# Banks from the waves' tiles, whole copies of the weights across halves, batch 3's turnings two waves later, and sums over x in two groups, in a polysketch-attention and GLU kernel

## Chip, cores and metric

The kernel runs on one core of a Trainium2 chip. The metric is the device time of one execution in microseconds (us). The median of three runs of the kernel before is 292.66 us (291.77 to 294.08).

## The reference

Four batches of four heads, 1088 positions, head width 32, fp32. Attention without a softmax over sketched features, and then a gated feed-forward block on the result:

```
def phi(x):
    a = np.einsum('rd,bhsd->bhsr', S1, x)
    b = np.einsum('rd,bhsd->bhsr', S2, x)
    return np.einsum('bhsi,bhsj->bhsij', a, b).reshape(*x.shape[:-1], r * r)
q_p, k_p = (phi(q), phi(k))
kv = np.einsum('bhsf,bhsd->bhfd', k_p, v)
z = np.sum(k_p, axis=2)
num = np.einsum('bhsf,bhfd->bhsd', q_p, kv)
den = np.einsum('bhsf,bhf->bhs', q_p, z)[..., None] + 1e-06
...
gate = 1.0 / (1.0 + np.exp(-(x @ w_gate)))
val = x @ w_val
return (gate * val @ w_out).astype(np.float32)
```

x is the attention's output `num / den`, 4352 tokens of 128 features; `w_gate` and `w_val` are 128 x 1536, `w_out` is 1536 x 128.

## The kernel before

**Tokens and waves.** x lies transposed in on-chip memory as `xT` (128 features x 4352 tokens), cut into eight chunks of 512 tokens and one of 256. Chunks 0 to 4 are done in 60 *waves*, twelve a chunk, numbered 0 to 59. A wave (`w1`, L615) multiplies one chunk by 128 columns of the gate weights and 128 of the value weights: eight TensorE records (L630) into one accumulation tile `wave` of 128 x 2 x 512 (two banks: bank 0 holds the gate, bank 1 the value). ScalarE takes the sigmoid of bank 0 (`sg`, L638) and VectorE multiplies it with bank 1 (`g`, L665). The product with `w_out` is done for chunks 1 to 4 in seven products instead of eight (Strassen's way), two waves later and more: `w2_a` and `w2_b` (their matmuls have line L478, as all that go through `product`), which need sums over tokens that GpSimd makes (`token_sums`, L468). There are two `wave` tiles, so the wave after next waits until this one's `g` is done.

**Attention beside the waves.** The attention of batches 1 to 3 is laid between the waves by hand. `slot()` issues one wave, `until(n)` issues waves until number n, and `plan[b]` (L1416) holds for batch b the wave numbers at which its twelve steps are issued: the turnings of k and q (`turn_k`, L725, and two of `turn_q`), the sketches (`begin`, whose first matmuls are `kps`, L756), the outer products, sums for z, `kv_all`, the denominators and `parts`, which writes x of that batch (`xT`, L1367). `begin` also spreads the features over partitions by a long ladder of transfers on SyncE's queue (`a<-dq`, `b<-dq`, L948), each of which is issued when the transfer eight before it has landed. Other small work hangs on `moe["prep"]`, a list of (wave, function) popped in order after each wave.

**Weights across.** `cross_weights` (L414) makes the weight combinations for the seven-product form of the first products. It copies pieces of the gate and value weights from one half of the partitions to the other, in seven transfers of 192 KB on ScalarE's queue (`fw<-w_sb`, L446, at `LOAD_AT`), and then adds and subtracts on VectorE (L441, at `SUM_AT`). It is called after wave 22, when the counter stands at 23, so that every entry up to 23 is popped at one time, after wave 23.

**The section.** Chunks 5, 6 and 7 are the *section* (`section()`, L1468): also the gate and value products are done in seven products there. Before it, x is loaded into `yt` with both halves on both halves of the partitions (`load_y`, four transfers of 128 KB on SyncE's queue, L1456) and four differences over x are made on GpSimd (`x_sum`, L1466); for chunk 5 that is at waves 54 and 56 to 59. `section` closes the pools of the wave tiles (four banks) and of a tile `two` (two banks) and opens a pool `pg` with six tiles of one bank, b0 to b5. Six gated pairs a chunk, 18 in all (w = 0 to 17), even and odd ones in their own banks: GA = b0 and b4, GC = b1 and b5, V = b2 and b3. The work is written out by hand as a string `ORDER` of 698 items, issued from left to right:

- `P1:w` to `P7:w`, and with an apostrophe for the second 128 columns: the seven products of pair w. P1 and P2 add into GA, P5 and P3 into GC, P6, P7 and P4 into V. Each uses half of TensorE's rows.
- `Aa`, `Ac` (ScalarE, L1555 and L1557) copy GA into V and GC into `s5`; `Sa`, `Sc` (ScalarE, L1559, L1561) are the sigmoids of GA and GC; `D1` adds V and `s5` into GC, `D2` adds V and `s5` into `c2` (VectorE, L570); `M1`, `M2` multiply V and `c2` with the sigmoids (VectorE, L1567, L1569). In pair w: P1 (both) before Aa; P5 (both) before Ac; Aa before P6; P6 before D1; P2 before Sa; P7 before D2; P3 and D1 before Sc; P4 before M1.
- `Q`: GpSimd's sums of g over tokens (L1582). `T`: differences over x for the next chunk. `WLA`, `WUA`, `WLB`, `WUB`: products with `w_out` on the lower or upper half of the rows; `WF` on all of them.
- `EA`, `EB` (L1584): ScalarE copies a finished accumulation bank (L1593), and five transfers on SyncE's queue (L1595 to L1600) move quarters of it. `F0` to `F5` add them up, `F6` turns and stores (L490).
- `C`, `Y`, `Z`, `O`: the last chunk of 256 tokens: C the products (Y reads GA, Z reads GC), Y the sigmoid (L1632), Z the multiplication (L1634), O the product with `w_out`.

The program is run in the order in which it is written; each engine takes its own instructions in that order, and what an instruction waits for on other engines is worked out by the compiler from the tiles that it reads and writes.

Of the kernel before, what the change touches and what calls it, by code (L numbers as in the profile page):

```python
# [16 lines left out]
P = 128  # L17

ORDER = """
P1:1 P1:0 T2:1 P1':0 WUB:-2.0 P5:1 WLA:-2.1 P5:0 P1':1 Aa:0 P5':0 P5':1 Aa:1 P2':0 P6':0 P2:0 P6:0  # L20
Ac:0 P6':1 P2:1 Ac:1 D1:0 P2':1 P6:1 Sa:1 D1:1 P3:0 P7:0 P3':0 P7':0 Sa:0 P7':1 P3':1 D2:0 T0:1 P7:1
P3:1 P1:2 P4':0 Sc:1 D2:1 P1':2 P4:0 Sc:0 P4:1 P1:3 M1:0 P1':3 P4':1 P5':3 P5':2 Aa:2 M1:1 P5:3
WLA:-1.1 P6:2 P5:2 M2:0 Aa:3 P6':2 P2:2 Ac:2 P2:3 P6':3 Q0:0 P6:3 WUB:-1.1 Ac:3 D1:2 WLA:-1.0
WUB:-1.0 Q1:0 D1:3 P2':3 WLA:-2.0 P2':2 P7':2 Sa:3 M2:1 P3:2 P7:2 Sa:2 P3':3 P3':2 D2:2 Q0:1 P3:3
P7':3 Sc:2 P1:5 P7:3 Q1:1 Sc:3 P4:2 P1':4 D2:3 P1:4 P4':2 Q2:0 P5:4 P1':5 M1:2 P4':3 WUA:-1.0 Q2:1
WUA:-2.1 P4:3 M2:3 Aa:4 P5':5 P5':4 WLB:-1.1 P6:4 M1:3 Q0:3 Ac:4 P2':4 P6':4 Aa:5 WUA:-1.1 WLB:-2.0
Q3:1 D1:4 P2:4 WUA:-2.0 P5:5 P6:5 M2:2 T1:1 EA:-1 P6':5 P7:4 Sa:4 P7':4 P3:4 Q0:2 P2':5 P3':4 Ac:5
D2:4 P2:5 P1:6 Q3:0 Sc:4 WLB:-1.0 WUA:1.1 D1:5 P4':4 P1':6 Sa:5 Q1:2 M2:4 P4:4 P5:6 EB:-1 P7:5
WUA:0.0 Q1:3 M1:4 P7':5 WUA:1.0 P5':6 P3':5 Q2:3 D2:5 Aa:6 P3:5 WLB:1.0 WLB:0.0 WUA:0.1 Ac:6 T3:1
F0:-1 P6:6 P4:5 Sc:5 Q3:3 WLB:1.1 P6':6 P4':5 P1':7 D1:6 Q0:4 P2':6 P5':7 P2:6 P1:7 M1:5 Q2:2 P7:6  # L30
P3:6 M2:5 Aa:7 WLA:0.1 P7':6 Q3:2 P3':6 P5:7 Sa:6 F1:-1 P2:7 P6':7 Ac:7 D2:6 WUB:1.1 P6:7 T0:2 P1':8
P2':7 Sc:6 D1:7 P1:8 WUB:3.0 T2:2 Sa:7 WLA:1.0 P4:6 M2:6 P3':7 P7:7 T1:2 P7':7 P3:7 P4':6 WLA:3.1
Q1:4 Sc:7 D2:7 P1':9 WLA:0.0 WUB:0.0 P5':8 M1:6 P4:7 P1:9 Q0:6 M2:7 Aa:8 P4':7 P5:9 P5:8 WUB:1.0
Q0:5 M1:7 WLA:3.0 P5':9 Ac:8 WLA:1.1 P6:8 F2:-1 Q1:5 Aa:9 P6':8 WLA:2.0 WUB:3.1 WLA:2.1 Ac:9 D1:8
Q2:5 P6:9 P2':9 WUB:2.0 P6':9 Q2:4 P3:8 P7':8 D1:9 P7:8 P3':8 T3:2 P2':8 P2:9 Sc:8 D2:8 P7':9 P3':9
Q3:4 Sa:9 P3:9 P2:8 M2:8 P4':8 P7:9 Q0:7 Sa:8 WLB:3.1 P4:8 D2:9 Sc:9 WUA:2.0 WLB:2.0 Q3:5 P1:10
WUA:2.1 M1:8 Q1:7 P4:9 P5:11 M2:9 P4':9 P5':11 P1:11 P1':10 M1:9 WLB:5.0 WUA:3.1 Aa:10 WLB:4.0
WUA:3.0 F3:-1 Ac:11 P5':10 P1':11 F4:-1 P5:10 P6:10 Aa:11 WUA:5.1 WLB:3.0 Ac:10 P6':10 WLB:5.1 Q0:9
P6':11 WUA:4.1 D1:10 WUA:4.0 P2:10 Q2:7 P2':10 WUA:5.0 F5:-1 P6:11 P7':10 Q1:6 Sa:10 P3:10 P7:10
D1:11 P2':11 P3':10 Q3:7 P1:12 WUB:5.1 D2:10 Sc:10 WUB:4.0 P7:11 Q1:9 P2:11 P7':11 M2:10 Q2:6 P4':10  # L40
WLA:5.0 Sa:11 P4:10 WLA:4.0 D2:11 WUB:5.0 WLA:5.1 Q3:6 M1:10 P1:13 WLA:4.1 EB:0 P3:11 P4':11 Q0:10
EA:0 P3':11 P4:11 WUB:7.1 P1':12 Sc:11 M1:11 Q1:10 WUB:6.0 P5':12 Aa:12 P1':13 P5:12 M2:11 Q2:9
P5:13 WLA:6.0 Aa:13 P6:12 WLA:7.1 F6:-1 Q3:9 Ac:12 WLA:7.0 P6':12 P5':13 WLA:6.1 Q0:8 D1:12 P6:13
P2':13 Ac:13 WUB:7.0 P6':13 F0:0 Q0:11 P3':12 P7':12 D1:13 P3:12 P7:12 Q2:10 P2:12 P2:13 Sc:12 D2:12
P3:13 P2':12 Q3:10 Sa:13 P3':13 P7':13 M2:12 P7:13 P4:12 Q1:11 Sa:12 WLB:6.0 P4':12 D2:13 Sc:13
WUA:6.0 WLB:7.1 Q1:8 WUA:6.1 P1:14 M1:12 WUA:7.1 P4':13 Q2:8 M2:13 P4:13 P5':15 P1':14 P1:15 Q2:11
M1:13 P1':15 P5':14 Aa:14 WUA:9.0 WLB:7.0 Q3:11 F1:0 Aa:15 P5:14 WUA:10.0 WLB:10.0 P6:14 Q3:8 Ac:14
P2:14 P6':14 P5:15 P6:15 D1:14 P6':15 WUA:9.1 Ac:15 WUA:7.0 P2':14 F2:0 P3:14 P7:14 D1:15 Sa:14
Q0:13 P7':14 P3':14 WUA:8.0 WLB:11.1 Q0:12 Sc:14 D2:14 WLB:9.1 WUA:8.1 WUA:11.1 WLB:11.0 Q1:13 M2:14
WLB:9.0 P4:14 WLB:8.0 P4':14 Q2:13 WUA:10.1 P7':15 M1:14 P3':15 P7:15 Q1:12 WUA:11.0 P1':16 D2:15  # L50
P5:16 P3:15 Q2:12 P2':15 P1:16 F3:0 Sc:15 P2:15 P4':15 F4:0 Q3:12 WUB:8.0 P4:15 F5:0 Sa:15 P5':17
WLA:8.0 Q3:13 Aa:16 WUB:9.1 WLA:8.1 WLA:9.0 P5:17 M1:15 P6:16 P5':16 Ac:17 WLA:10.0 P6':16 M2:15
Ac:16 WLA:11.1 P1:17 P1':17 WLA:9.1 D1:16 WUB:9.0 WLA:11.0 Aa:17 WUB:11.0 WLA:10.1 Q0:15 P3':16
P7':16 EA:1 P6:17 P7:16 Q1:15 P2:17 P6':17 D2:16 P3:16 WUB:10.0 Q0:14 P2':16 P2':17 D1:17 Sc:16
P2:16 P4:16 Q2:15 P4':16 WLA:12.0 M2:16 Sa:16 P7:17 WUB:11.1 Q1:14 Sa:17 P3':17 WLA:13.0 M1:16 P3:17
P7':17 Q0:16 C1:0 Sc:17 D2:17 Q2:14 C0:0 C3:0 M2:17 Y:0 Q1:16 C2:0 EB:1 C1:1 Z:0 Q0:17 P4:17
WUA:13.0 WLB:12.0 WUA:13.1 Q2:16 F6:0 WUA:12.0 WLB:13.1 WUA:12.1 WLB:13.0 Q3:14 F0:1 C0:1 Q3:16 C3:1
F1:1 Y:1 C2:1 F2:1 Q3:15 C3:2 Z:1 C0:2 C2:2 C1:2 C0:3 Y:2 WUB:13.1 P4':17 WUB:12.0 WLA:12.1 M1:17
WUB:13.0 WLA:13.1 Z:2 C1:3 Q1:17 C3:3 Y:3 C2:3 Q2:17 F3:1 WFA:16.0 Z:3 WFA:15.1 Q3:17 WFA:15.0
WFA:16.1 F4:1 WFA:14.1 F5:1 WFA:17.1 WFA:14.0 F6:1 WFA:17.0 WFB:15.0 EA:2 WFB:17.1 WFB:14.0 WFB:16.0  # L60
WFB:17.0 WFB:15.1 C1:5 EB:2 C0:5 F0:2 C2:5 Y:5 C3:5 F1:2 O3:3 C3:4 Z:5 O1:1 C2:4 O2:2 C1:4 F2:2 O2:1
O0:5 F3:2 O1:2 O0:3 F4:2 C0:4 F5:2 O3:2 O2:3 Y:4 O3:0 O1:0 F6:2 O0:0 O3:5 O2:5 Z:4 O0:1 O1:3 O1:5
O3:1 O0:2 O2:0 O1:4 O0:4 O2:4 O3:4
# [4 lines left out]
def kernel(  # L68
# [23 lines left out]
    SECT, HELD, BUF = 5, 2, 0  # L92
    LOAD_AT, SUM_AT = (19, 19, 20, 20, 22, 22, 23), (24, 25, 25, 30, 30, 31, 32, 34, 34, 37)
# [16 lines left out]

    pso = ctx.enter_context(tc.tile_pool(name="pso", bufs=1, space=bass.MemoryType.PSUM))
    early = ctx.enter_context(ExitStack())
    psm = early.enter_context(tc.tile_pool(name="psm", bufs=2, space=bass.MemoryType.PSUM))
    ps2 = early.enter_context(tc.tile_pool(name="ps2", bufs=1, space=bass.MemoryType.PSUM))
# [298 lines left out]

    def cross_weights():  # L414
# [5 lines left out]
        loads, sums = [], []  # L420
        for turn in range(2):
# [4 lines left out]
            for dst, src in ((lead, tail), (tail, lead)):  # L426
                if turn == 0 or dst == lead:
                    loads.append((f[0][dst], g[src]))
                loads.append((f[2][dst], v[src]))
# [17 lines left out]
        for at, many in ((LOAD_AT, loads), (SUM_AT, sums)):  # L447
            for n in at:
                moe["prep"].append((n, many.pop(0)))
            assert not many  # L450
        moe["prep"].sort(key=lambda x: x[0])
# [965 lines left out]
    plan[3] = (44, 45, 45, 46, 47, 48, 49, 51, 54, 55, 56, 58)  # L1417
# [28 lines left out]
    YT = {}  # L1446

    def load_y(c):
        t = sbA.tile([P, 2 * H * W1], F32, tag="qp", name="yt")
        y = t[:, : 2 * TCH].rearrange("p (k t) -> p k t", k=2)  # L1450
        s = t[:, 2 * TCH : 4 * TCH].rearrange("p (u t) -> p u t", u=4)
        YT[c] = y, s
        t0 = tok_chk[SECT + c][0]
        for k, src in enumerate((LO, HI)):
            for dst in (LO, HI):
                nc.sync.dma_start(out=y[dst, k], in_=xT[src, t0 : t0 + TCH])  # L1456

    def x_sum(c, u):
        y, s = YT[c]
        out, in0, in1 = (  # L1460
            (s[:, 0], y[:, 0, HALF:], y[:, 0, :HALF]),
            (s[:, 1], y[:, 1, HALF:], s[:, 0]),
            (s[:, 2], y[:, 1, HALF:], y[:, 0, HALF:]),
            (s[:, 3], y[:, 1, :HALF], s[:, 1]),
        )[u]
        nc.gpsimd.tensor_tensor(out=out, in0=in0, in1=in1, op=ALU.subtract)  # L1466

    def section():  # L1468
# [3 lines left out]
        early.close()  # L1472
        pg = ctx.enter_context(tc.tile_pool(name="pg", bufs=1, space=bass.MemoryType.PSUM))
        bank = [pg.tile([P, TCH], F32, tag=f"b{x}", name=f"b{x}") for x in range(6)]
        GA, GC, V = (bank[BUF], bank[4]), (bank[BUF + 1], bank[5]), (bank[2 - BUF], bank[3 - BUF])
# [108 lines left out]
        def empty(b, c):  # L1584
# [8 lines left out]
            nc.scalar.copy(out=e, in_=acc[b, c])  # L1593
            if b == "A":
                nc.sync.dma_start(out=x1[LO], in_=e[HI, :HALF])  # L1595
                nc.sync.dma_start(out=x1[HI], in_=e[LO, :HALF])
            else:
                nc.sync.dma_start(out=x2[LO], in_=e[HI, HALF:])
                for rows in (LO, HI):
                    nc.sync.dma_start(out=x5[rows], in_=e[LO, HALF:])  # L1600
# [53 lines left out]
        for item in ORDER.split():  # L1654
# [21 lines left out]
            else:  # L1676
                gated(k, n)
        store_end(acc["end"])

    at = NJ * SECT  # L1680
    until(at - 6)
    load_y(0)
    for u in range(4):
        until(at - 4 + u)
        x_sum(0, u)
    until(at)
    glu()
    if SECT + 1 < len(tok_chk) - 1:
        load_y(1)
# [33 lines left out]
```

## Time and profile before

| What | Value |
|---|---|
| median of three runs | 292.66 us (291.77 to 294.08) |
| profiled execution: its own time | 293.18 us |
| its span in the profile | 291.2 us |
| mean granted TensorE clock | 0.994 |
| TensorE busy | 279.6 us, 96% of the span, 3204 matmuls |
| VectorE busy | 212.1 us, 73% |
| GpSimd busy | 178.5 us, 61% |
| ScalarE busy | 119.4 us, 41% |
| section: first product to the end of the last stage's products | 183.77 to about 287.8 us |

Between span and own time lie 2.0 us outside the profile. In the timeline views the columns are start, duration, engine, line, operation, output and inputs, shapes, count; a bracket at the end gives the idle time of that engine before the row and what ended it. In the groups of operations, the columns after the bar are busy time, mean ns of one, and the idle time before them with its releasers.

### The profile page before, as it was taken

How to read it: one execution, taken by the hardware profiler on the slowest of the kernel's cores; microseconds unless marked ns; L12 is line 12 of the kernel's file. 1: busy time of each engine (PE TensorE's matmuls, PEld its weight loads, DVE VectorE, ACT ScalarE, POOL GpSimd, SP SyncE). 2: the span in 40 equal slices, each digit the busy share in tenths (PEclk: the TensorE clock that was granted, in tenths of full speed). 3: DMA queues.
4: the chain of work that ended last, by engine and by line, in shares of the span. 5: the costliest groups of instructions: out<-in, count | busy, mean ns of one | idle time of the engine just before them, and what ended most of it. 6: DMA issues, size and time to landing. Idle time of an engine off the chain costs nothing.

```text
span 291.2 us, 7846 instructions
## 1 busy us (share of the span) xinstructions
PE 279.6 (96%) x3204; PEld 158.4 (54%) x3204; DVE 212.1 (73%) x342; ACT 119.4 (41%) x231; POOL 178.5 (61%) x234
## 2 busy tenths in 40 slices
PE   8899999999979999999999999899999999999985
PEld 3554433454423445544344544488887887766654
DVE  6986788955739899787866557477888777867643
ACT  3798732322323322443225223566554464452111
POOL 2666682766445769763586656727969797675300
PEclk9999999999998999999999999999999999999999
DMA  7995441867480267415076530200310031003033
GB/s 221 346 350 124 103 154 43 197 145 196 103 185 0 38 164 166 143 39 171 4 179 158 122 57 10 64 3 8 76 42 0 5 69 18 2 20 64 13 73 55
DMA packets 32916, 28.63 MB, mean 98 GB/s; under 512 B 19184, under 2 KB 27312, under 8 KB 32880
## 3 DMA queue, kind: packets, MB, share of 16 engines
q1 hardware_dynamic: 28448, 24.98, 34.1%
q10 hardware_dynamic: 4432, 3.15, 4.3%
q8 instruction: 25, 0.41, 0.6%
q14 instruction: 11, 0.09, 0.1%
HBM read 20.60 MB, written 3.26 MB: 82 GB/s over the span
## 4 chain that ended last, share of the span: by engine, by line
PE 85%; DVE 7%; DMA 3%; issue 2%; ACT 1%; POOL 1%; ACTq 1%; SPq 0%; DVEq 0%
PE wave L630 32%; PE b L478 22%; PE prod L478 20%; PE moeout L522 4%; DVE rb L1356 1%; DVE xT L1367 1%; DMA fw<-w_sb 1%; PE kvz L975 1%; DVE g L665 1%; PE nps L1333 1%; PE kps L756 1%; PE moeout L478 1%; DMA s_in<-in_S_dram 1%; DVE kT L725 1%; DMA xb<-e 1%
## 5 line engine op out<-in xcount | busy, mean ns | idle before, releaser
L630 PE MATMUL wave<-xT,w_sb 128*64 128x512 f32 (+2 forms) x436 | 120.5, 598 | 2.8 <-DVE g L665 2.7
L478 PE MATMUL prod<-tsum,ws 64*64 64x256 f32 (+1 forms) x348 | 82.8, 379 | 0.0
L638 ACT ACTIVATE sg<-wave 128x512 f32<-128x512 f32 x60 | 35.7, 597 | 96.1 <-PE wave L630 84.9
L630 PEld LDWEIGHTS wave<-xT,w_sb 128*64 128x64 f32 (+1 forms) x436 | 41.4, 144 | 49.4 <-issue 35.5
L478 PE MATMUL b<-yt,fw 64*64 64x256 f32 x792 | 64.1, 377 | 1.4 <-DVE g L665 1.4
L468 POOL TENSOR_TENSOR tsum<-g,tsum 128x256 f32<-128x256 f32 x48 | 44.8, 933 | 33.7 <-DVE g L665 33.4
L665 DVE TENSOR_TENSOR g<-wave,sg 128x512 f32<-128x512 f32 x60 | 41.0, 683 | 25.1 <-ACT sg L638 25.1
L478 PE MATMUL prod<-g,w_sb 64*64 64x256 f32 (+2 forms) x234 | 55.2, 377 | 0.0
L468 POOL TENSOR_TENSOR tsum<-g 128x256 f32<-128x256 f32 x48 | 41.8, 871 | 19.2 <-DVE g L665 19.0
L478 PEld LDWEIGHTS b<-yt,fw 64*64 64x64 f32 x792 | 42.3, 133 | 12.3 <-DVE g L665 2.3
L478 PEld LDWEIGHTS prod<-tsum,ws 64*64 64x64 f32 (+1 forms) x348 | 42.8, 135 | 8.4 <-issue 4.3
L1582 POOL TENSOR_TENSOR tsum<-g 128x256 f32<-128x256 f32 x36 | 27.8, 786 | 20.3 <-DVE g L1569 14.2
L478 PEld LDWEIGHTS prod<-g,w_sb 64*64 64x64 f32 (+1 forms) x234 | 26.1, 135 | 18.3 <-issue 13.7
L478 PE MATMUL prod<-tsum,w_sb 64*64 64x256 f32 (+1 forms) x116 | 33.3, 379 | 0.0
L478 PE MATMUL prod<-g,ws 64*64 64x256 f32 (+1 forms) x116 | 33.3, 378 | 0.0
L1582 POOL TENSOR_TENSOR tsum<-g,tsum 128x256 f32<-128x256 f32 x36 | 28.7, 807 | 1.0
L478 PE MATMUL b<-yt,w_sb 64*64 64x256 f32 x216 | 25.6, 377 | 0.0
L570 DVE TENSOR_TENSOR b<-b,s 128x512 f32<-128x512 f32 x18 | 12.5, 698 | 10.1 <-PE b L478 9.1
L478 PEld LDWEIGHTS prod<-g,ws 64*64 64x64 f32 (+1 forms) x116 | 15.4, 135 | 4.5
L570 DVE TENSOR_TENSOR c<-b,s 128x512 f32<-128x512 f32 x18 | 12.4, 689 | 5.9 <-PE b L478 5.7
L478 PEld LDWEIGHTS prod<-tsum,w_sb 64*64 64x64 f32 (+1 forms) x116 | 15.3, 136 | 1.3 <-POOL tsum L1582 0.5
L1555 ACT COPY b<-b 128x512 f32<-128x512 f32 x18 | 10.3, 575 | 14.1 <-PE b L478 8.1
(162 smaller groups left out, 386.6 us busy)
## 6 DMA issues: line engine op xcount, KB each, us to landing
qp<-dq SPq DMA_DIRECT2D x7, 576.0 KB, 8.2
bq<-dq SPq DMA_DIRECT2D x14, 288.0 KB
kq<-in_k_dram SPq DMA_DIRECT2D x3, 544.0 KB
kq<-in_q_dram SPq DMA_DIRECT2D x3, 544.0 KB, 4.8
w_in<-in_moe_w_out_dram SPq DMA_DIRECT2D x6, 256.0 KB
yt<-xT SPq DMA_DIRECT2D x12, 128.0 KB, 2.3
fw<-w_sb ACTq DMA_DIRECT2D x7, 192.0 KB
w_in<-in_moe_w_gate_dram SPq DMA_DIRECT2D x5, 256.0 KB, 5.5
```

Source lines behind the costliest of these rows:

```text
L468: nc.gpsimd.tensor_tensor(out=t[:, u], in0=in0, in1=in1, op=ALU.subtract)
L478: nc.tensor.matmul(out=out, lhsT=lhsT, rhs=rhs, start=start, stop=stop, skip_group_check=True)
L522: nc.tensor.matmul(out=moe["acc"][d], lhsT=w_sb[:, 2, j, d], rhs=g[:, jj], start=(j == 0), stop=(j == NJ - 1),)
L570: nc.vector.tensor_tensor(out=out, in0=in0, in1=in1, op=ALU.add)
L630: nc.tensor.matmul(out=wv[d, which, jj * tw + o : jj * tw + o + tp], lhsT=w_sb[:, which, j0 + jj, d], rhs=xT[:, t0 + o : t0 + o + tp], sta ...
L638: nc.scalar.activation(out=sg, in_=wv[:, 0], func=ACTF.Sigmoid)
L665: nc.vector.tensor_tensor(out=g, in0=wv[:, 1], in1=sg, op=MUL)
L725: nc.vector.transpose(out=kT_of[b][:, t0:t1].rearrange("p t s -> p (t s)"), in_=k_t[b][:, t0:t1].rearrange("p t d -> p (t d)"),)
L756: nc.tensor.matmul(out=ts[pi][32 * g : 32 * g + 32, : NJK * 32], lhsT=sk[rows, :], rhs=kT_of[b][rows, KBASE[g] : KBASE[g] + NJK], start=Tr ...
L975: nc.tensor.matmul(out=kvz[32 * h : 32 * h + 32, :F], lhsT=v_sb[:, h, j, :], rhs=KP[b][:, h // 2, j, h % 2, :], start=(j == 1), stop=(j == 0),
L1555: nc.scalar.copy(out=v, in_=ga)
L1582: nc.gpsimd.tensor_tensor(out=t[:, out], in0=in0, in1=in1, op=ALU.subtract)
```

## The change

- **Copies across.** Four whole copies of 64 partitions x 6 KB (384 KB each) take the place of seven of 192 KB. `LOAD_AT` is (19, 20, 23, 24): three are issued together after wave 23 and one after wave 24.
- **Banks.** The two wave tiles and the tile `two` are kept to the end, and the section takes its six banks as halves of these three two-bank tiles: GA0 and GC0 are the halves of one tile, V0 and V1 of the second, GA1 and GC1 of the third. The pool `pg` is gone.
- **Batch 3's plan.** `turn_k` two waves later, the following steps by two, two, one, two, two, two, two, none, none, one and none.
- **x's differences.** `load_y(0)` after wave 47 instead of at wave 54; the differences 0 and 1 after wave 53, 2 and 3 after wave 57, instead of one each at waves 56 to 59. They hang on `moe["prep"]` now.
- **Last transfers.** The five transfers of `EA:2` and `EB:2` go to ScalarE's queue.
- **Order.** `ORDER` has the same 698 items in another order.

```diff
-    SECT, HELD, BUF = 5, 2, 0
-    LOAD_AT, SUM_AT = (19, 19, 20, 20, 22, 22, 23), (24, 25, 25, 30, 30, 31, 32, 34, 34, 37)
+    SECT, HELD = 5, 2
+    LOAD_AT, SUM_AT = (19, 20, 23, 24), (24, 25, 25, 30, 30, 31, 32, 34, 34, 37)
+    XPLAN = ((47, None), (53, (0, 1)), (57, (2, 3)))
...
+    psm = ctx.enter_context(tc.tile_pool(name="psm", bufs=2, space=bass.MemoryType.PSUM))
     pso = ctx.enter_context(tc.tile_pool(name="pso", bufs=1, space=bass.MemoryType.PSUM))
-    early = ctx.enter_context(ExitStack())
-    psm = early.enter_context(tc.tile_pool(name="psm", bufs=2, space=bass.MemoryType.PSUM))
-    ps2 = early.enter_context(tc.tile_pool(name="ps2", bufs=1, space=bass.MemoryType.PSUM))
+    ps2 = ctx.enter_context(tc.tile_pool(name="ps2", bufs=1, space=bass.MemoryType.PSUM))
...
-        loads, sums = [], []
+        loads = [
+            (fw[0][dst, k], w_sb[src, i])
+            for k, i in ((2, 1), (0, 0)) for dst, src in ((LO, HI), (HI, LO))
+        ]
+        sums = []
...
-            for dst, src in ((lead, tail), (tail, lead)):
-                if turn == 0 or dst == lead:
-                    loads.append((f[0][dst], g[src]))
-                loads.append((f[2][dst], v[src]))
...
+        for n, group in XPLAN:
+            moe["prep"].append((n, lambda group=group: load_y(0) if group is None else [x_sum(0, u) for u in group]))
         moe["prep"].sort(key=lambda x: x[0])
...
-    plan[3] = (44, 45, 45, 46, 47, 48, 49, 51, 54, 55, 56, 58)
+    plan[3] = (46, 47, 47, 47, 49, 50, 51, 53, 54, 55, 57, 58)
...
-        early.close()
-        pg = ctx.enter_context(tc.tile_pool(name="pg", bufs=1, space=bass.MemoryType.PSUM))
-        bank = [pg.tile([P, TCH], F32, tag=f"b{x}", name=f"b{x}") for x in range(6)]
-        GA, GC, V = (bank[BUF], bank[4]), (bank[BUF + 1], bank[5]), (bank[2 - BUF], bank[3 - BUF])
+        bank = [psm.tile([P, 2, 512], F32, tag="wave", name="b") for _ in range(2)]
+        bank.append(ps2.tile([P, 2, 512], F32, tag="two", name="b"))
+        bank = [x[:, u] for x in bank for u in range(2)]
+        GA, GC, V = (bank[0], bank[4]), (bank[1], bank[5]), (bank[2], bank[3])
...
+            eng = nc.scalar if c == chunks - 1 else nc.sync
...
-                nc.sync.dma_start(out=x1[LO], in_=e[HI, :HALF])
-                nc.sync.dma_start(out=x1[HI], in_=e[LO, :HALF])
+                eng.dma_start(out=x1[LO], in_=e[HI, :HALF])
+                eng.dma_start(out=x1[HI], in_=e[LO, :HALF])
...
-    at = NJ * SECT
-    until(at - 6)
-    load_y(0)
-    for u in range(4):
-        until(at - 4 + u)
-        x_sum(0, u)
-    until(at)
+    until(NJ * SECT)
```

The pairs 10 and 11 as `ORDER` has them, from P1:11 on, before and after:

```diff
-P1:11 P1':10 M1:9 WLB:5.0 WUA:3.1 Aa:10 WLB:4.0
-WUA:3.0 F3:-1 Ac:11 P5':10 P1':11 F4:-1 P5:10 P6:10 Aa:11 WUA:5.1 WLB:3.0 Ac:10 P6':10 WLB:5.1 Q0:9
-P6':11 WUA:4.1 D1:10 WUA:4.0 P2:10 Q2:7 P2':10 WUA:5.0 F5:-1 P6:11 P7':10 Q1:6 Sa:10 P3:10 P7:10
-D1:11 P2':11 P3':10 Q3:7 P1:12 WUB:5.1 D2:10 Sc:10 WUB:4.0 P7:11 Q1:9 P2:11 P7':11 M2:10 Q2:6 P4':10
...
+P1:11 WUA:4.1 P1:10 Q1:8 M1:9 P1':10 P1':11 P5:11 P5':10 F2:-1 Q2:7 Aa:10 P5:10
+WUA:3.0 F3:-1 Aa:11 WUA:3.1 WLB:5.0 Q3:7 F4:-1 P6:10 P2:10 Ac:10 P6':10 WLB:5.1 Q2:6 P6:11 P5':11
+D1:10 WUA:5.0 WLB:4.0 Q0:9 Ac:11 WUA:5.1 P6':11 F5:-1 P7':10 P3':10 T1:2 D1:11 P7:10 P3:10 P2':11
+P2':10 Q1:9 Sc:10 D2:10 P2:11 P7:11 Sa:10 P7':11 P3:11 T3:2 M2:10 P4:10 WLA:5.1 Sa:11 Q3:6 P4':10
+WLA:5.0 D2:11 P3':11 WLA:4.0 Q2:8 WLA:4.1 WUB:4.0 M1:10 Sc:11 P4':11 WUB:5.1 EA:0 P4:11 WUB:5.0
...
```

## The prediction

> **What bounds the kernel now.** I read the busy times first (TensorE 279.6 of 291.2 us), then TensorE's waits by cause. They are few, and none of the larger ones lies in the middle of the section:
>
> ```profile
> PE wave L630 <- DVE g L665: 2.7, 2, 2.1
> PE b L478 <- DVE g L665: 1.4, 1, 1.4
> PE moeout L478 <- DVE g L1634: 1.4, 1, 1.4
> ```
>
> (Total us, times, longest.) So a stall put into TensorE's stream is paid in full. The windows view (busy us, granted clock) gives each stage:
>
> ```profile
> 82.00:86.20 4.20, 2.06 (x14) 1.00 1.07 223
> 86.30:89.70 3.40, 3.40 (x10) 0.50 0.01 2
> 180.00:183.77 3.77, 2.36 (x12) 1.00 0.50 113
> 183.77:281.39 97.62, 97.55 (x1620) 1.00 0.15 29
> ```
>
> The section's 97.6 us have 0.07 us of idle. Wave 26 waits 2.14 us and then runs at clock 0.50 for 3.4 us. The timeline has the rows behind that wait (the copies, the sigmoid after a sum, g), and further on the two rows that matter most here:
>
> ```profile
> 78.57 5.61 ACTq L446 DMA_DIRECT2D fw<-w_sb  x7
> 84.28 1.08 ACT L638 ACTIVATE sg<-wave 128x512 f32<-128x512 f32 x2 [5.18 <-DMA fw<-w_sb]
> 84.59 0.96 DVE L441 TENSOR_TENSOR fw<-w_sb,fw 128x768 f32<-128x768 f32 x1 [4.76 <-DMA fw<-w_sb]
> ...
> 152.01 1.89 PE L630 MATMUL wave<-xT,w_sb 128*64 128x512 f32 x8
> ...
> 153.95 0.60 ACT L638 ACTIVATE sg<-wave 128x512 f32<-128x512 f32 x1 [1.98 <-PE wave L630]
> ```
>
> The sigmoid reads bank 0 of the wave tile, written by the first half of the eight records, by about 153.1. It starts at 153.95, when bank 1 is written too: a tile of two banks is waited for as a whole. The section's own steps take, after the tile is complete:
>
> ```profile
> L1561 ACT ACTIVATE sg<-b 128x512 f32<-128x512 f32 x18 | 10.6, 598 | 11.8 <-PE b L478 11.8
> L1555 ACT COPY b<-b 128x512 f32<-128x512 f32 x18 | 10.3, 575 | 14.1 <-PE b L478 8.1 <-DVE g L1567 6.0
> ```
>
> VectorE's additions there take 0.69 to 0.70.
>
> **The change part by part**
>
> *Banks and order* (cost about 43). The new section takes its banks as halves of two-bank tiles. By the rows above each half then waits for work on the other. The compiled program of the changed kernel says so: of 469 waits between engines in the section 190 join instructions that touch different banks of one tile; before, 0 of 450. Example: Aa:10 copies GA0, complete after P1':10, but it waits for P5':10, which writes GC0 and stands right ahead of it; the next product P5:10 writes GC0 and waits for Aa:10. TensorE has nothing between. The stall is 0.21 (a product's last matmul to ScalarE's start, 184.70 to 184.91 in the timeline) + 0.575 (the copy) + 0.05 (end to TensorE's next start, as 187.86 to 187.92) = 0.83 us. With other steps (0.57 to 0.70) the same sum is 0.83 to 0.96; I use 0.86. Products on half of the rows cost 0.215 us each, as two run side by side (eight in 1.72), so four items between cover 0.86.
>
> I counted, at every product that waits for a ScalarE or VectorE step, the TensorE items since the product that feeds that step. Before, none of 76 such waits has fewer than four. After, 53 of 83 have: 13 have none between, 24 one, 10 two, 6 three. 13 x 0.86 + 24 x 0.645 + 10 x 0.43 + 6 x 0.215 = 32.3 us. Counting overlapping ones once, but including chains in which one step waits for another, gives 31 to 34 us in 57 stalls.
>
> This leaves out that a late step makes the next one late, so I walked two stretches by hand with the written order, the compiled waits and those durations. From P1:11 to the next P1':13, 43 items = 9.2 us took 12.4: stalls at P5:10 (Aa:10) 0.83, P6':11 (D1:10) 0.53, P7:10 (D1:11) 0.96, P7:11 (D2:10) 0.52, P4':11 (M1:10) 0.77, less what rounding gives back: 3.2. From P5':8 to P4':9, 53 items = 11.4 us took 17.8: nine stalls, 6.4 (the largest at P7:7, M1:6, and P2:9, D1:9, 0.96 each). Together 9.6 us over 96 items, 0.10 an item. The section has 364 half-row items: 36.4. The stage of C, Y and Z has six such waits of about 0.85 (GA and GC are one tile, so Y waits for all four products): 5.1. After a stall TensorE needs about 0.05 to fill: 57 x 0.05 = 2.9. Sum 44.4. The section already loses about 2.8 us besides its tail gap (from 183.77 to 287.8 are 104.0 us; its work is 99.8 and the gap 1.4), from half-row items without a partner; a stall lets the halves line up again, so I take off half of that, 1.4. **+43.0**; the ends are 31 (each stall once, nothing passed on) and 51 (the second walk's 0.12 an item, +7.6).
>
> [...]
>
> *Copies across* (−1.5). Wave 26 waits for g of wave 24, which stands behind the first sum (L441, 84.59) on VectorE; and that wave's sigmoid stands behind the issuing of seven copies on ScalarE, until 84.2. Three copies take about 2 us to issue (0.6 to 0.7 each there), so the sigmoid is early and only the sum is late. The first sum needs the first two new copies, 768 KB; the old ones moved some 200 to 215 GB/s from 79.7 to 86.4 (1344 KB). From 79.9 that lands near 83.7 instead of 84.4; the sum ends near 84.8, g near 85.5, and 0.7 of the 2.14 us go. Then the clock: 3.41 us at half speed cost 1.71, and I take half of it, 0.8, as gone. Ends: 0 (total bytes grow to 1536 KB, so nothing is earlier) and −3.85 (wait and low clock both gone).
>
> *Batch 3's turnings* (−0.6). VectorE's 1.30 us turn at 138.86 stands behind batch 2's xT (138.12 and 138.73) and ahead of g, which ends at 140.74; the wave behind waits 0.57. Two waves on, xT is long done and the turn runs beside the wave. Ends −0.6 and 0.
>
> *x's loads and differences* (+3.4). SyncE's queue issues `yt<-xT` behind the `a<-dq`, `b<-dq` ladder, which took from 142.66 (`kps`) to 163.88 and begins one wave (2.6 us) later now, although the step is written at wave 47. So the loads land near 167 to 169, and the two differences written after wave 53 block GpSimd until then, ahead of the token sums of the pair 52 and 53, which `w2_a` needs before wave 56. With two differences of 0.9 and the sums of 0.73 each I get about 2.5 us on TensorE, and 0.9 for a lower clock after an idle time like that at 84. Ends 0 (loads land in time) and +4.2 (as large as 2.5 and the whole 1.71).
>
> *Entry into the section* (−1.2). Now 1.41 us idle at 182.36 wait for g(59), behind two xT operations of 1.24 and 1.10 us, which took 0.69 when GpSimd was idle (138.12). In the new program P1:0 takes the tile of wave 58 and waits only for that g; and two differences fewer run beside xT. Ends −1.4 and 0.
>
> *Last transfers* (−1.4). Eight stores hold SyncE's queue from 274.30 to 278.06, so EA:2's transfers are issued at 278.16, F0 runs at 280.85, Z at 281.65, and the products behind it wait 1.37 at 281.39. ScalarE's queue has no stores there, but the issues now take its time, 0.5 to 0.6 each: EA:2 and two of them (1.7 us) ahead of Y:2 lie beside four products of 0.43, EB:2 and three (2.4) ahead of Y:5 beside 2.8 us of products. So they are just covered; without that cover they would cost up to 1. Ends −1.4 and +1.
>
> Sum: +43.0 − 1.5 − 0.6 + 3.4 − 1.2 − 1.4 = +41.7, on 293.18 of the profiled execution 334.9. That execution is 0.5 above the median of the runs, so 334.4; I say **334**.
>
> **The rivals**
>
> *Not slower* (5%). The waits bind less than I read, because TensorE's queue reaches the waiting product later than its predecessors were done. All then hangs on one figure: four items, 0.86 us; where TensorE is that far behind, a wait costs nothing. It would leave the smaller terms: −1.5 − 0.6 + 3.4 − 1.2 − 1.4 = −1.3, 291.9; without GpSimd's stall 288.5. For it: 30 of the 83 waits are covered so. Against it: 37 have one item or none between, and the 0.05 us after VectorE's end at 187.86 shows the next product following its releaser at once.
>
> *Stalls overlap* (20%). Each is paid once and passes nothing on, as the two halves of the rows run on independently up to the wait: 31 − 1.4 in the section and −1.3 for the rest, 293.2 + 28.3 = 321.5; with no stall on GpSimd 318.
>
> *The clock falls* (12%). The stalls add up to a low clock in parts of the section. One such phase cost 1.71 us at 86.3 to 89.7; eight of them 13.7: 348. For it: the phase after 2.14 us of idle. Against it: idles of 1.41 and 1.37 us brought none (clock 1.00 and 0.99 in the last windows), and my stalls are under 1 us each.
>
> [...]
>
> **How the numbers follow.** My forecast, near 334 with its own range 326 to 343, has 63%. The range reaches down to 319 (stalls once, small GpSimd stall) and up to 349 (second walk's density, or the clock). About 1% is what a measurement of this kernel can tell from no change, 2.9 us. Faster by more than that needs the first rival without GpSimd's stall: 3%. Within it 2%. Slower 95%.
>
> **What would show each step.** Banks: TensorE's waits named `b <- ACT b`, `b <- ACT s`, `b <- ACT sg`, `b <- DVE b`, some 50 to 60 in all, each 0.4 to 1.0 us, summing to 30 to 45; busy time hardly changed. Copies: the idle before wave 26 near 1.4. x's differences: a wait of TensorE for `tsum` near 160 to 170, with `yt<-xT` issued just before. Entry: no 1.4 us ahead of the section. Tail: F0 within 2 us of the copies. The forecast is wrong if waits for ScalarE and VectorE in the section are few or far shorter than 0.4 us; then the section's waits are met before TensorE arrives.

## The result, and the profile after

The changed kernel takes 345.4 us (median of 4 runs, 342.3 to 348.6) against 292.6 us before: ratio 1.176, 95% interval 1.167 to 1.186. Ratios here and below are of mean times, without executions more than 1.5% above the fastest of their kernel (one of these four, three of the ten of own_banks below). The profiled execution took 342.26 us, the fastest of the four, with a span of 340.2, which is 49.0 longer than the 291.2 of before; the prediction's sum of +41.7 is compared with this difference. The profiled execution had a mean granted clock of 1.000. The other three had 0.995, 0.989 and 0.979, with spans of 343.7, 343.2 and 346.5; they left no trace, so where their clock fell is not known.

The page of the changed kernel, its span, busy times and TensorE's row of the 40 slices; below it the same row of the kernel before:

```profile
span 340.2 us, 7848 instructions
PE 301.9 (89%) x3204; PEld 153.7 (45%) x3204; DVE 211.8 (62%) x342; ACT 120.0 (35%) x231; POOL 174.8 (51%) x234
PE   9899999999899999999899877766889787977895
```

```profile
PE   8899999999979999999999999899999999999985
```

The matmuls are as many as before. ScalarE and VectorE are as busy as before, in a longer time. TensorE is at 6 to 9 tenths in the second half, where it stood at 9 nearly throughout. And its *busy* time has grown by 22.3 us as well.

TensorE's waits by cause in the changed kernel (total us, times, longest):

```profile
PE b L502 <- ACT b L1557: 6.8, 13, 0.9
PE b L502 <- DVE b L594: 6.3, 11, 0.9
PE b L502 <- DVE g L1569: 4.8, 7, 1.0
PE b L502 <- ACT sg L1635: 2.8, 4, 0.7
PE b L502 <- ACT sg L1563: 2.6, 4, 0.8
PE wave L654 <- DVE g L689: 2.3, 2, 1.9
PE prod L502 <- POOL tsum L492: 1.8, 1, 1.8
PE b L502 <- ACT s L1559: 1.6, 4, 0.8
PE b L502 <- DVE c L594: 1.6, 3, 0.8
```

Where the section had two waits of any size, ahead of its first product and at the last products, it has some fifty, none above 1.0 us, on every kind of ScalarE and VectorE step (`b`, `s`: the copies; `sg`: the sigmoids; `b`, `c`: the additions; `g`: M1). They are the waits that the prediction named.

The chain of waits that sets the end, in a stretch of 6 us of the section (start, duration, what):

```profile
237.58 0.60 ACT sg L1563
238.18 0.04 issue
238.23 0.66 PE b L502 x8
238.89 0.43 PE prod L502 x8
239.32 0.47 PE b L502 x8
239.80 0.02 issue
239.82 0.58 ACT b L1557
240.40 0.04 issue
240.44 0.43 PE b L502 x2
```

Before, the chain ran through TensorE's own instructions there. Now it changes engines: products, the copy Aa:8 (239.82), and at 240.44, 0.04 us after the copy, P4:7. The two have nothing to do with each other: Aa:8 writes V0, P4:7 adds into V1, the other half of the tile.

The section's products as one window (length, TensorE's busy time, records, clock), first the kernel before, then the changed one:

```profile
183.77:287.78 104.01, 102.57 (x1704) 1.00 0.16 31
```

```profile
183.19:336.73 153.54, 125.11 (x1704) 1.00 0.11 21
```

The section takes 49.5 us more at full clock, so the clock has no part in it. The remaining 49.0 − 49.5 = −0.5 is −0.6 ahead of it and +0.1 behind it. Idle gaps between its products (over 0.1 us) number 50 and make 28.2 us, against one of 1.4; TensorE's busy time has grown by 125.1 − 102.6 = 22.5.

### The profile page after: what moved, and what is told of

Its sections match the earlier page's. It is cut to its first block, busy times and chain, and to the rows that moved or that the text cites. A ratio compares the mean times of both kernels' runs of the same rounds, so it can differ in the third digit from the quotient of the medians.

```text
span 340.2 us, 7848 instructions
## 1 busy us (share of the span) xinstructions
PE 301.9 (89%) x3204; PEld 153.7 (45%) x3204; DVE 211.8 (62%) x342; ACT 120.0 (35%) x231; POOL 174.8 (51%) x234
## 4 chain that ended last, share of the span: by engine, by line
PE 70%; DMA 9%; DVE 8%; ACT 6%; issue 3%; SPq 1%; POOL 1%; ACTq 0%; DVEq 0%; POOLq 0%
PE b L502 25%; PE wave L654 24%; PE prod L502 13%; DMA bq<-dq 4%; PE moeout L546 3%; ACT b L1557 3%; DVE b L594 3%; DMA fw<-w_sb 2%; DVE g L1569 2%; DMA v<-in_v_dram 2%; ACT s L1559 1%; DVE c L594 1%; PE nps L1357 1%; DMA kq<-in_k_dram 1%; PE moeout L502 1%
## 5 line engine op out<-in xcount | busy, mean ns | idle before, releaser
L654 PE MATMUL wave<-xT,w_sb 128*64 128x512 f32 (+2 forms) x436 | 118.3, 590 | 2.4 <-DVE g L689 2.3
L502 PE MATMUL b<-yt,fw 64*64 64x256 f32 x792 | 77.3, 387 | 18.0 <-ACT b L1557 6.8
L1584 POOL TENSOR_TENSOR tsum<-g 128x256 f32<-128x256 f32 x36 | 27.7, 783 | 71.1 <-PE prod L502 37.0
L492 POOL TENSOR_TENSOR tsum<-g,tsum 128x256 f32<-128x256 f32 x48 | 46.0, 957 | 29.1 <-DVE g L689 28.8
L502 PEld LDWEIGHTS b<-yt,fw 64*64 64x64 f32 x792 | 36.6, 132 | 47.8 <-ACT b L1557 11.7
L492 POOL TENSOR_TENSOR tsum<-g 128x256 f32<-128x256 f32 x48 | 40.6, 846 | 20.0 <-DVE g L689 19.7
L502 PEld LDWEIGHTS prod<-tsum,ws 64*64 64x64 f32 (+1 forms) x348 | 40.5, 135 | 13.0 <-issue 6.2
L502 PE MATMUL b<-yt,w_sb 64*64 64x256 f32 x216 | 28.0, 386 | 6.2 <-DVE b L594 2.6
L502 PEld LDWEIGHTS prod<-g,w_sb 64*64 64x64 f32 (+1 forms) x234 | 24.3, 134 | 15.7 <-issue 10.7
L1584 POOL TENSOR_TENSOR tsum<-g,tsum 128x256 f32<-128x256 f32 x36 | 26.5, 747 | 1.1
L594 DVE TENSOR_TENSOR c<-b,s 128x512 f32<-128x512 f32 x18 | 12.4, 690 | 15.9 <-PE b L502 15.9
L1569 DVE TENSOR_TENSOR g<-b,sg 128x512 f32<-128x512 f32 x18 | 12.4, 689 | 14.7 <-PE b L502 12.6
L1557 ACT COPY b<-b 128x512 f32<-128x512 f32 x18 | 10.3, 571 | 30.9 <-PE b L502 22.1
L1563 ACT ACTIVATE sg<-b 128x512 f32<-128x512 f32 x18 | 10.8, 598 | 29.2 <-PE b L502 29.2
```

The lines of the kernel that those rows point to most:

```text
L492: nc.gpsimd.tensor_tensor(out=t[:, u], in0=in0, in1=in1, op=ALU.subtract)
L502: nc.tensor.matmul(out=out, lhsT=lhsT, rhs=rhs, start=start, stop=stop, skip_group_check=True)
L594: nc.vector.tensor_tensor(out=out, in0=in0, in1=in1, op=ALU.add)
L654: nc.tensor.matmul(out=wv[d, which, jj * tw + o : jj * tw + o + tp], lhsT=w_sb[:, which, j0 + jj, d], rhs=xT[:, t0 + o : t0 + o + tp], sta ...
L1557: nc.scalar.copy(out=v, in_=ga)
L1563: nc.scalar.activation(out=sg[:, :, second], in_=two(gc), func=ACTF.Sigmoid)
```

## The experiments

**own_banks: the changed kernel with six tiles of one bank.**

```diff
-        bank = [psm.tile([P, 2, 512], F32, tag="wave", name="b") for _ in range(2)]
-        bank.append(ps2.tile([P, 2, 512], F32, tag="two", name="b"))
-        bank = [x[:, u] for x in bank for u in range(2)]
+        early.close()
+        pg = ctx.enter_context(tc.tile_pool(name="pg", bufs=1, space=bass.MemoryType.PSUM))
+        bank = [pg.tile([P, TCH], F32, tag=f"b{x}", name=f"b{x}") for x in range(6)]
```

(and the pools psm and ps2 closed ahead of it, as before.)

> The changed kernel with six tiles of one bank in the section, everything else as changed. Theory (waits on whole tiles): of the 55 places where fewer TensorE items stand between a step and the product behind it than the step takes, one is left; the section goes back from 154 us to about 104, and the time to 290 to 293. Rival (the new order is to blame, whatever the tiles are): the section stays above 120 us and the time above 310.

Measured: 293.34 us (median of 10 runs, 291.1 to 296.5), ratio to the kernel before 0.998 (0.995 to 1.002). Its section as one window, and TensorE's waits above 0.9 us in the whole kernel:

```profile
185.42:287.10 101.68, 101.67 (x1700) 1.00 0.15 30
```

```profile
PE wave L655 <- DVE g L690: 2.3, 2, 1.9
PE prod L503 <- POOL tsum L493: 1.6, 1, 1.6
PE kps L781 <- DVE sk L1263: 1.0, 1, 1.0
```

Every wait inside the section is gone with one edit. The same order of work takes 101.7 us, less than the 104.0 of the kernel before (one product of four records, WUB:-2.0, now stands ahead of this window); the tiles cost 153.5 − 101.7 = 51.9 us. The order is not to blame.

**before_shared: the kernel before with shared tiles.** The opposite edit: the pools and the three lines of the change's banks put into the kernel before.

> The kernel before with its section's banks taken as halves of three two-bank tiles, as in the change; order, copies, plan and the rest as before. Theory (whole tiles): 53 stalls whose lengths, counted from the spacing, sum to 30 us, about as in the changed kernel (55 and 31), plus what each drags along (in the changed kernel 19 us in 55): about 340. Rival (the order): below 300.

Measured: 342.47 us (4 runs), ratio 1.171 (1.166 to 1.175); 54 gaps of 28.5 us in its section. An order made for tiles of one bank loses nearly as much with shared tiles as the new one (49.3 us against 51.9 in the section), so the two orders are alike in this. The theory holds from both sides.

**v_shared, g_shared, v_pair, by_kind: which sharing, and how much.** In own_banks, only V of the even and odd pair become halves of one tile (v_shared), or only GA and GC of a pair (g_shared):

```diff
-        bank = [pg.tile([P, TCH], F32, tag=f"b{x}", name=f"b{x}") for x in range(6)]
-        GA, GC, V = (bank[0], bank[4]), (bank[1], bank[5]), (bank[2], bank[3])
+        bank = [pg.tile([P, TCH], F32, tag=f"b{x}", name=f"b{x}") for x in range(4)]
+        both = pg.tile([P, 2, TCH], F32, tag="bv", name="bv")
+        GA, GC, V = (bank[0], bank[2]), (bank[1], bank[3]), (both[:, 0], both[:, 1])
```

> The changed kernel with only V of the even and odd pairs in one two-bank tile, GA and GC in tiles of their own. By the spacing 26 stalls of 14.5 us in all. If each stall drags along some 0.35 us of TensorE halves working alone, 292 + 14.5 + 9 = 316; if a stall costs only itself, 306; if the order is to blame, as the changed kernel.

> The changed kernel with only GA and GC of one pair in one two-bank tile, V in tiles of their own. By the spacing 28 stalls of 14.0 us in all. With 0.35 us dragged along by each: 292 + 14 + 10 = 316; with nothing dragged along 306.

In these two V stands in the banks of the former tile `two`, and what they compute is off by 6%; the instructions and their order are the same, so they serve for the time alone. v_pair is v_shared with V where the second wave tile had been, which keeps the whole computation:

```diff
-        bank = [pg.tile([P, TCH], F32, tag=f"b{x}", name=f"b{x}") for x in range(4)]
+        bank = [pg.tile([P, TCH], F32, tag=f"b{x}", name=f"b{x}") for x in range(2)]
         both = pg.tile([P, 2, TCH], F32, tag="bv", name="bv")
+        bank += [pg.tile([P, TCH], F32, tag=f"b{x}", name=f"b{x}") for x in (2, 3)]
```

> As v_shared (only V of the even and odd pairs in one tile), with this tile in the banks that the second wave tile had. The waits are the same, so 325 to 329 as v_shared; if the place of the banks mattered, another time.

by_kind is the changed kernel with another use of the same halves:

```diff
-        GA, GC, V = (bank[0], bank[4]), (bank[1], bank[5]), (bank[2], bank[3])
+        GA, GC, V = (bank[0], bank[1]), (bank[4], bank[5]), (bank[2], bank[3])
```

> The changed kernel with the same three two-bank tiles, but the halves given to the even and the odd pair: GA of both in one, V of both in the second, GC of both in the third. Fewer false waits: by the spacing 41 stalls of 23.6 us in all, against 55 and 30.9. In the four kernels so far the section lost, beyond the counted length, 0.36, 0.38, 0.42 and 0.70 us a stall. By that it loses 39 to 52 us here and the time is 330 to 343. If tiles shared within a pair are what hurts, it is near 300.

Measured, one run each of these four, in the order of the heading: 326.92, 320.64, 327.47 and 332.27 us. v_pair and by_kind came out within their ranges; v_shared and g_shared took more than the 316 that had been expected at most of the tiles. g_shared loses 25.7 us in the section, where 24 were expected, and starts it 2.3 later than own_banks. v_shared loses 32.7 in the section, where 23.5 were expected. The table sets the stalls counted from the spacing beside the gaps over 0.1 us that the traces have in the section, and what the section takes beyond the 101.7 us of own_banks (before_shared: beyond the 104.0 of the kernel before):

| Kernel | counted stalls, us | gaps seen, us | section, us | beyond | beyond counted, a stall |
|---|---|---|---|---|---|
| own_banks | 1, 0.1 | 0 | 101.7 | | |
| g_shared | 28, 14.0 | 26, 13.2 | 127.4 | 25.7 | 0.42 |
| v_shared, v_pair | 26, 14.5 | 31, 17.3 in both | 134.4 | 32.7 | 0.70 |
| by_kind | 41, 23.6 | 41, 24.6 | 144.2 | 42.5 | 0.46 |
| before_shared | 53, 30 | 54, 28.5 | 153.3 | 49.3 | 0.36 |
| changed kernel | 55, 30.9 | 50, 28.2 | 153.5 | 51.9 | 0.38 |

The number of places with too few items between step and product gives the number of gaps within five; by_kind came out where the earlier rows put it. What was open is the last column: each stall drags along some 0.4 us more than its counted length (0.36 to 0.46), and 0.70 where V alone is shared. Why V's stalls drag along more is not shown. With every tile shared between the pairs (by_kind) the loss is 42.5, with GA and GC shared within a pair and V between (the change) 51.9; so neither kind of sharing is harmless. The place of the banks changes nothing (v_pair: 134.4 us in the section, as v_shared).

Where those 0.4 us go can be read in a timeline of the changed kernel, between two stalls:

```profile
242.25 0.38 PE L502 MATMUL b<-yt,fw 64*64 64x256 f32 x2
242.26 0.38 PE L502 MATMUL prod<-g,ws 64*64 64x256 f32 x1
242.27 0.38 PE L502 MATMUL prod<-tsum,ws 64*64 64x256 f32 x1
242.47 0.60 PE L502 MATMUL b<-yt,fw 64*64 64x256 f32 x4
243.11 0.57 ACT L1557 COPY b<-b 128x512 f32<-128x512 f32 x1 [2.72 <-PE b L502]
243.73 0.43 PE L502 MATMUL b<-yt,fw 64*64 64x256 f32 x2 [0.67 <-ACT b L1557]
```

At 242.25 both halves of the rows work (two records of `b`, two of `prod`). From 242.47 four records of `b` run alone: the product for the other half stands behind P5':9, which waits for Aa:9. So half of TensorE has nothing for 0.43 us before the gap begins, and all of that counts as busy. Records of one half start 0.215 to 0.216 us apart in the unbroken stream. Taking 0.2125 us from each record's start as its time on its half, by estimate only one half works during about 23.5 us of the changed kernel's section and 1.5 of own_banks'; half of the difference, about 11.0 us, is lost so, 0.22 a gap. The rest of the growth in busy time (125.1 − 101.7 − 11.0 = 12.4, or 0.25 a gap) is mainly the run-out of the last records, which take 0.38 to 0.43 us where the next ones start after 0.215; in an unbroken stream the next record covers that. A smaller part is the restart: behind a gap the second records of a half start 0.27 after the first (243.73 and 244.00), 0.05 later than in the stream.

**copies_only: the four whole copies in the kernel before.**

```diff
-    LOAD_AT, SUM_AT = (19, 19, 20, 20, 22, 22, 23), (24, 25, 25, 30, 30, 31, 32, 34, 34, 37)
+    LOAD_AT, SUM_AT = (19, 20, 23, 24), (24, 25, 25, 30, 30, 31, 32, 34, 34, 37)
...
+        loads = [
+            (fw[0][dst, k], w_sb[src, i])
+            for k, i in ((2, 1), (0, 0)) for dst, src in ((LO, HI), (HI, LO))
+        ]
```

> The kernel before with the four whole copies alone. The prediction has -1.5 us (ratio 0.995). Since then the changed kernel's trace shows the wait of wave 26 only 0.25 shorter and a new wait of 0.40 behind it, and the kernel before with shared banks waited 2.17 there without the half clock: by that the copies themselves are worth about nothing and the ratio is 0.999 to 1.001, the 0.9 us that the changed kernel has gained there being the clock's.

Measured: 293.02 us (12 runs), ratio 1.002 (1.001 to 1.003): no gain, rather a small loss, and above both expectations. The timeline of the changed kernel shows why there is no gain:

```profile
84.58 0.96 DVE L463 TENSOR_TENSOR fw<-w_sb,fw 128x768 f32<-128x768 f32 x1 [4.51 <-DMA fw<-w_sb]
...
86.19 1.94 PE L654 MATMUL wave<-xT,w_sb 128*64 128x512 f32 x8 [1.89 <-DVE g L689]
...
89.39 1.94 PE L654 MATMUL wave<-xT,w_sb 128*64 128x512 f32 x8 [0.40 <-DVE g L689]
```

The first sum starts at 84.58, where it started at 84.59. Counted from the first copy's issue (78.81, before 78.57) that is only 0.25 sooner, although it waits for two of the four copies. So the wait is 0.25 shorter, and 0.40 come back at the next wave, behind the second sum. The 0.9 us that the changed kernel is ahead after this place come from the clock, which fell to 0.50 in the profiled execution of the kernel before and stayed at 1.00 here: before_shared, with the seven copies, a wait of 2.17 and clock 1.00, is 0.96 ahead at the same place. The trace of copies_only has the clock of 1.00 too, and its section begins 0.83 us earlier than in the kernel before. Of this 0.50 is given back in the section, 0.41 of it in one wait at 238.65, and 0.46 behind the last products; whether the copies have to do with that is not shown.

**plan_x: batch 3's plan and x's loads and differences in the kernel before**, with the change's three edits for them (plan[3], `XPLAN`, the loop ahead of the section gone).

> The kernel before with batch 3's plan and x's loads and differences moved as in the change, nothing else. From the wave times of the changed kernel: the turning -0.8, two differences ahead of the token sums +1.8 to +2.1, entry into the section between -1.2 and 0 (with tiles of its own): 0 to +1.3 us, ratio 1.000 to 1.004. The prediction's terms give -0.6 + 3.4 - 1.2 = +1.6, ratio 1.005. If x's loads cost nothing: -0.8 to -2.

Measured: 297.52 us (4 runs), ratio 1.018 (1.016 to 1.020), worse than every expectation. One of its waits and two windows of 2 us behind it (clock in the column behind the records):

```profile
PE prod L504 <- POOL tsum L494: 3.9, 1, 3.9
```

```profile
172.00:174.00 2.00, 1.23 (x6) 0.74 0.01 2
174.00:176.00 2.00, 2.00 (x6) 0.50 0.00 0
```

The starts of the waves (their records one by one, against the kernel before) say the rest: after the turning they are 0.79 earlier, and between the 400th and the 416th record of 436 they lose 5.85: 3.94 of waiting, and 1.9 behind it, where the clock was low. The entry into the section keeps its 1.41 with tiles of one bank.

In the changed kernel the same wait was 1.83. GpSimd's rows and SyncE's queue there:

```profile
164.60 2.95 SPq L424 DMA_DIRECT2D yt<-xT  x4
...
168.15 0.72 POOL L434 TENSOR_TENSOR yt<-yt 128x256 f32<-128x256 f32 x1 [4.50 <-DMA yt<-xT]
...
169.49 0.72 POOL L434 TENSOR_TENSOR yt<-yt 128x256 f32<-128x256 f32 x1 [0.61 <-DMA yt<-xT]
...
170.94 0.43 PE L502 MATMUL prod<-tsum,ws 128*64 128x256 f32 x1 [1.83 <-POOL tsum L492]
```

The loads written at wave 47 are issued at 164.60, behind the ladder's last transfer (164.19). GpSimd stands 4.5 us at the first difference until they land, with the token sums behind it.

**later_sums: own_banks with these two differences after wave 55.**

```diff
-    XPLAN = ((47, None), (53, (0, 1)), (57, (2, 3)))
+    XPLAN = ((47, None), (55, (0, 1)), (57, (2, 3)))
```

> The changed kernel with tiles of one bank (as own_banks) and the first two differences over x after wave 55 instead of 53. If their wait for x's loads, ahead of the token sums on GpSimd, is the cause of the 1.6 us wait of TensorE near 172, that wait goes and the kernel is 1.6 to 1.8 us faster than own_banks: ratio to the kernel before about 0.992. Rival: the differences then hold up later token sums or the entry into the section, and the ratio stays at 0.998.

Measured: 289.27 us (5 runs), ratio 0.990 (0.988 to 0.991), faster than both kernels. The wait for `tsum` is gone from TensorE's list, and nothing took its place; past the start of the kernel, the two waits of wave tiles (1.9 and 0.4) and 0.8 ahead of the section are what is left of any size. The span is 3.3 us shorter than that of own_banks: 1.8 as forecast at this place, and 1.5 at the start of the kernel, where the first wave of own_banks came later; there the edit changes nothing.

**tail_only: the last five transfers on ScalarE's queue in the kernel before** (the lines of the change for them).

> The kernel before with the last chunk's five transfers on ScalarE's queue alone. Prediction: the wait of 1.4 us ahead of the last products goes, ratio 0.995. Rival: issuing takes ScalarE's time ahead of the sigmoids and gives it back, ratio 1.000.

Measured: 291.93 us (12 runs), ratio 0.997 (0.995 to 0.999). The wait ahead of the last products is 0.40 in place of 1.37:

```profile
281.11 0.88 PE L478 MATMUL moeout<-w_sb,g 128*64 128x128 f32 x12 [0.40 <-DVE g L1635]
```

Z still is a little late, because issuing (0.61, 0.47 and two in 1.20) stands ahead of the sigmoid on ScalarE. So the gain is 0.3%, between prediction and rival; with the new order the wait is gone altogether.

**seven_copies: later_sums with the seven copies of before.**

> later_sums with the seven copies of the kernel before in place of the four. copies_only was 0.2% slower than the kernel before, so this is 0.2% faster than later_sums: 288.7, ratio 0.988. If the copies only moved with the clock, as later_sums: 0.990.

Measured: 290.19 us (5 runs), ratio 0.990 (0.988 to 0.992): the same as later_sums, as the second of the two expectations had it. The intervals are too wide to confirm or to refute the 0.2% of copies_only.

## Why the prediction was right, and which of its terms was mis-sized

It gave 334, range 319 to 349; the profiled execution, on which the sum was made, took 342.3 instead of 334.9. The direction, the mechanism and the place were right. The median of the runs, 345.4, is 3 us higher still; in those executions the clock was lower somewhere. Term by term, from the starts of the wave records and the section's windows:

| Term | predicted | measured |
|---|---|---|
| banks and order, in the section | +43.0 | +51.9 (own_banks to the changed kernel) |
| last transfers, and the order without its waits | −1.4 | −2.3 (kernel before to own_banks, some 0.2 of it the product now ahead of the window) |
| copies across | −1.5 | −0.9, as much as the clock of 1.00 alone gave before_shared |
| batch 3's turning | −0.6 | −0.8, and −0.1 behind it |
| x's loads and differences | +3.4 | +2.1 (5.9 in plan_x) |
| entry into the section | −1.2 | −1.1 |
| start of the kernel | none | +0.2 |
| sum | +41.7 | +49.0 |

- **Waits on whole tiles** were read off the sigmoid that waits for both banks (it starts at 153.95, 0.05 us after the eighth record's end at 153.90) and off the compiled waits. own_banks and before_shared show it as cause from both sides: the program waits on the other half of a tile too, and in the section that costs 51.9 us with the new order and 49.3 with the old one.
- **The walks by hand** held in the main. From the start of P1:11 to that of P1':13 12.4 us were forecast and 13.1 measured (9.5 in own_banks), from P5':8 to P4':9 17.8 and 20.0 (11.2 in own_banks). So the two lost 12.4 us against own_banks, where the walks had 9.6.
- **The step that was mis-sized** is the sentence "a stall lets the halves line up again, so I take off half of that, 1.4". The halves do not line up; they lose their partner: +11.0 in place of −1.4. The idle that was forecast (36.4 + 5.1 + 2.9 = 44.4, which includes each last record's run-out) came out at 28.2 in gaps and 12.4 in run-out, 40.6. So the stalls themselves cost 4 us less and the lone halves 12 us more, which leaves 8.6 of the 8.9 that the term was short. That the term came this close is in part luck: two errors of opposite sign offset each other.
- **The range's upper end** held for another reason than it named: it was built on the second walk's density and on low clocks, and in the profiled execution the section ran at clock 1.00. The measured 51.9 lies just beyond the 51 that the prediction gave as the upper end of this term.
- **The signs.** The waits came as named: 50 gaps (forecast 50 to 60 waits), none above 1.0 us, 28.2 us in sum (forecast 30 to 45). "Busy time hardly changed" was wrong, it grew by 22.3 us. The idle ahead of wave 26 was 1.89, not near 1.4. F0 of the last chunk began 2.8 us behind its copy (326.73 and 323.91), not within 2, and the wait of the last products was gone all the same.
- **Copies:** the first two copies were priced as if they had the rate of the transfers to themselves, to land near 83.7; the sum that waits for them started at 84.58. All four had landed by 86.35, where the next sum starts, so by estimate they share the rate; that was not tested by itself.
- **x's loads:** the mechanism was right to the instruction (the ladder, the two differences, the token sums, the product). The size is not fixed: TensorE waited 1.6 us in own_banks, 1.8 in the changed kernel, 3.3 to 3.6 in v_shared, g_shared and v_pair and 3.9 in plan_x. The traces show what goes with it. VectorE multiplies 128 x 1152 numbers there (`qp<-qp,bq`, at 170.38 in the changed kernel), and one GpSimd instruction that runs beside it takes 1.8 to 1.9 us in place of 0.72. In own_banks, the changed kernel and by_kind (1.8 too) the sum that TensorE waits for begins before that (170.17), and the slow one is the next (170.85). In v_shared, g_shared and v_pair the loads land 0.2 to 0.7 later against the waves than in the changed kernel, the sum begins behind VectorE's start (v_shared: 170.39 and 170.35) and is the slow one itself. In plan_x the ladder ends at 165.77 in place of 164.19, and the second difference (1.37) is in the way. Neither this overlap nor why the ladder ends at other times was tried by itself.
- **The rivals.** "Not slower" fell: with shared tiles TensorE stood idle in 50 places. "Stalls overlap" fell: 321.5 forecast against 342.3; its 31 us of stalls, each paid once, stand against 40.6 of gaps and run-out. "The clock falls" fell for the section of the profiled execution. In the three others the mean clock was 0.979 to 0.995, so it may have a part in the 3 to 6 us that they took more. In other kernels it did show ahead of the section, at 0.50 behind some waits of 2.1 to 3.9 us.

## What to carry to other kernels

What the program waits for here is the tile, not the bank that is touched (50 gaps of 28.2 us in the section with shared tiles, none over 0.1 us in own_banks); where an order of work is written for single banks, give each bank a tile of its own, and read the compiled waits before believing the order. To price such a change, count the items between the product that feeds a step and the product that waits for it against the step's time, and add per stall the last record's run-out and the time in which one half of the rows waits for the other: here some 0.4 us on top of a counted 0.56 (30.9 in 55), and 0.7 in one of the kernels. A load that is written earlier is not issued earlier while its queue is held by a ladder of transfers (written at wave 47, it was issued from 164.60 on, behind the ladder's last transfer at 164.19; written at wave 54, in the kernel before, from 164.29 on), and the engine that waits for it stands with everything behind (GpSimd 4.50 us).

## What the runs showed that was not expected

- **The clock after an idle time varies.** Waits of 2.14 to 2.18 us ahead of wave 26 were followed by a clock of 0.50 in two executions (the kernel before, seven_copies) and by 1.00 in three (before_shared, tail_only, plan_x). Between the first 20 us of the kernel and its last products, waits of 1.9 or less lowered it in none, waits of 3.3 to 3.9 (v_shared, g_shared, v_pair, plan_x) in all four. Each time the clock stayed at 0.50 for 3.41 us (the windows of the six executions give 3.40 to 3.44). The price was 1.0 us behind wave 26's wait (the prediction had 1.7), and 1.9 in plan_x. Why the same wait goes both ways is not shown. A gain of 0.9 us beside such a wait can therefore be the clock's. Whether the four copies have a merit in it is open: with them the wait is 1.89 and the clock stayed at 1.00 behind it in all eight traces, with the seven it is 2.14 to 2.18 and the clock stayed in three of five. The mean clocks of the executions point the same way (0.998 to 1.000 in the five of later_sums, 0.993 to 0.998 in the five of seven_copies), but which wait lowered them is not known.
- **Busy time is not work.** The same 1700 records took 101.7 us of busy time in own_banks and 125.1 in the changed kernel, at the same clock.
